# Entering a batch's v tiles term by term, and zeros in planned gaps of the whole early phase, in a planned attention and gated-MLP kernel

## The chip, the core and the metric

One core of a Trainium2 chip. The time of a kernel is the device time in microseconds; several runs are shown by their median. The kernel before has 417.27 us (three runs, 416.51 to 417.78). A measurement of this kernel can tell about 0.3% from no change, which is 1.25 us.

## What is computed

Local and global attention, then a gated MLP on its output, in float32 for 4 batches, 8 heads of 64, 768 positions:

```python
scores = scale * np.matmul(q, k.transpose(0, 1, 3, 2))
scores = np.where(keep, scores + bias, -1e9)        # keep: 8 global keys, or the 96 before
a = np.exp(scores - scores.max(-1)); a = a / (a.sum(-1) + 1e-09)
x = heads_side_by_side(np.matmul(a, v))             # (B, 768, 512)
h = gelu(x @ w_in)                                  # tanh form, 1024 columns
u, v = h[..., :512], h[..., 512:]
v_n = (v - v.mean(-1)) / np.sqrt(v.var(-1) + 1e-06) * g_ln
v_s = np.einsum('ts,bsd->btd', w_sg, v_n) + b_sg[None, :, None]
out = x + (u * v_s) @ w_out
```

## The kernel before

**Attention** goes in units of one batch, one pair of heads and 256 positions: 12 units a batch, 48 in all, numbered from 0 in the order of `units` (256 positions first, then the four pairs). `step` issues for a unit: the scores of a unit three ahead (L831, in quarters of the array, into two PSUM banks `s_ps`), its softmax (`softmax`: DVE adds the bias and takes the extreme at L863, ACT takes the exponent at L868, DVE the reciprocal at L881, and the four parts of `p` are scaled at L888 on ACT, L890 on POOL or L893 on DVE), the transposes of `p` (for units below 16 on TensorE at L952, into the bank `tps`, copied to `pt` at L957 on ACT or L958 on DVE), the product with v (L980, banks `av`), and `take`, which copies `av` to `xh` (L1077) and splits it into a high and a low part of the tile `x` (L1089 to L1095). A unit fills the x of its pair of heads and its 256 positions.

**The MLP** multiplies in three terms (high by high, high by low, low by high), so that each product over 128 rows is three matmuls, L500, L501 and L502, from `Moe.terms`. Per batch there are six v tiles (128 positions by 512 columns, four products over the pairs of heads, 12 matmuls each, bank `mm_ps`), u tiles, mix tiles (w_sg by the normalised v, named `z`) and output tiles. Behind a v tile stands its gelu (`gelu2`: L519 on ACT, L521 on DVE, L523 on ACT, L524 on DVE), then the norm (L558 to L560 on DVE, L563 on POOL, L565 on DVE) and the split into `z` (L534 and L538). Weights come in 64-bit floats and are turned into pairs by `load_split` (L665 on ACT, L668 to L672 on DVE, L675 or L676, and L677).

**The order.** `phase` interleaves units with MLP tiles in source order; every operation goes to `Plan`, which tries 40 random sets of priorities against its own costs, gives each operation an engine (some can run on two or three) and a place, and writes the best order down engine by engine. What is emitted is a fixed order on each of PE, ACT, DVE, POOL and SP. A tile whose product waits for data at its first term only is set by `behind`: with 0, the first term waits for all pairs' x (L506 to L518). Batch 0 has three phases of four units: no tiles in the first, v tiles 0 and 1 in the second, 2 and 3 in the third; v tiles 4 and 5 lead the first phase of batch 1, followed by the u tiles and the mix tiles.

**Zeros.** Where the planner sees TensorE idle for 0.6 us or more ahead of an operation that opens a bank, before 29 us, `keep_on` (L443 to L450) multiplies zeros into that bank, as many as `zeros` works out from the planned gap. The zeros are read from the first part of `bsg`, the place of a bias vector, which is therefore loaded only after 30 us (`w.vectors.since`).

Of the kernel before, what the change touches and what calls it, by code (L numbers as in the profile page):

```python
# [13 lines left out]
BF16 = mybir.dt.bfloat16  # L14
# [5 lines left out]
P = 128  # L20
# [3 lines left out]
FF = 512  # L24
NT = S // P
KD = DM // P
# [31 lines left out]

APART = 0.2

IDLE, ON_UNTIL = 0.6, 29.0

SPARE, SPARE_LATE = 2, 0

# [147 lines left out]
class Plan:  # L212
# [231 lines left out]
    def keep_on(self, o):  # L444

        to = next((b for b in o.bufs if b.kind == "bank" and b.ops[0] is o), None)
        n = o.banks
        for _ in range(self.zeros(o)):
            self.tc.nc.tensor.matmul(to[:, 0:n], self.on[:, 0:P], self.on[:, 0:n], start=True,
                                     stop=True)  # L450

    def emit(self, start):
# [24 lines left out]
class Moe:  # L477
# [62 lines left out]
        op([on_dve_sb(n) + (lambda: lo(nc.vector),), on_pool(n) + (lambda: lo(nc.gpsimd),)],  # L540
           [src, (out, 0)], [(out, 1)])

    def v_tile(self, x, t):
        w = self.w
        c, ts = t * P // CH, ds(t * P % CH, P)
        return self.terms(
            KD, FF, lambda k: ((x[k][c][:, 0, ts], x[k][c][:, 1, ts]),
                               (w.win[:, 0, k, FF:], w.win[:, 1, k, FF:])),
            lambda k: [(x[k][c], t), (w.win, (k, 2))], 0, partial(self.norm, t))

    def norm(self, t, ps):
        nc, w, op = self.nc, self.w, self.plan.op
# [130 lines left out]
def local_global_attention_moe(tc, qk_in, v_in, q_t, k_t, v_n, n_gl, w_in, g_ln, w_sg_t, b_sg,  # L683
# [5 lines left out]
    w = Weights()  # L689
# [16 lines left out]
    w.g = wp.tile([P, KD], F32, name="g")  # L706
    w.bsg = wp.tile([P, S], F32, name="bsg")

    on = w.bsg.bitcast(BF16)[:, 0:FF]
    nc.vector.memset(on, 0.0)  # L710
    xp = fast.enter_context(tc.tile_pool(name="x", bufs=1))
    zp = fast.enter_context(tc.tile_pool(name="z", bufs=1))
# [389 lines left out]
    w.wsg = Buf(lambda _: wp.tile([P, 2, NT, S], F32R, name="wsg"))  # L1102
    w.wout = Buf(lambda _: wp.tile([P, 2, KD, DM], F32R, name="wout"))
    w.vectors = Buf(None)
    w.vectors.since = ON_UNTIL + 1.0

    def load_vectors():
        op([("SP", 0.38, 0.3, lambda: nc.sync.dma_start(
# [113 lines left out]
    def flat(*lists):  # L1222
        return [x for todo in lists for x in todo]
# [11 lines left out]
    for b in range(B + 1):  # L1235
        n0 = [(b * NU + u) * NPAIR for u in range(NU)]
        ns = [range(a, a + NPAIR) if b < B else [] for a in n0]
        if b < B:
            moe = Moe(nc, w, (zp, tp), bank, plan)
            x, dst = X(b), out[b]  # L1240
            cur = ([moe.v_tile(x, t) for t in range(NT)],
                   {(c, j): moe.u_tile(x, c, j) for c in range(NCH) for j in range(KD)},
                   {(c, j): moe.mix_tile(c, j) for c in range(NCH) for j in range(KD)},
                   [[moe.out_tile(x, c, m, dst, b == B - 1 and c == NCH - 1) for m in range(KD)]
                    for c in range(NCH)])
        if b == 0:
            phase(ns[0], [], w_v)
            load_vectors()
            phase(ns[1], flat(*cur[0][0:2]), w_u[:4])
            phase(ns[2], flat(*cur[0][2:4]), w_u[4:] + w_s[0][:3])  # L1250
        else:
            v, u, mix, o = prev
            lead = flat(v[4], v[5], u[0, 0], u[0, 1], mix[0, 0], u[0, 2], mix[0, 1], u[0, 3],
                        mix[0, 2], mix[0, 3])
            late = w_s[0][3:] + w_o[0] + w_o[1] + w_s[1] if b == 1 else []
            if b < B:
                phase(ns[0], lead + flat(u[1, 0], *o[0]), late)
                phase(ns[1], flat(u[1, 1], mix[1, 0], u[1, 2], mix[1, 1], u[1, 3], mix[1, 2],
                                  mix[1, 3]))
                phase(ns[2], between(cur[0][0:4], o[1]))  # L1260
            else:
                phase([], lead + flat(u[1, 0], *o[0], u[1, 1], mix[1, 0], u[1, 2], mix[1, 1],
                                      u[1, 3], mix[1, 2], mix[1, 3]))
                phase([], [t[k] for k in range(KD) for t in o[1][:3]] + o[1][3])
        prev = cur
        if b == 1:
            general = cp.tile([P, 1], I32, name="general")
            op([("DVE", 0.9, 1.0, find_general)], [xs[b, 0, 0]], [])
# [154 lines left out]
```

## Time and profile before

| | us |
|---|---|
| median of three runs | 417.27 |
| the profiled execution | 415.91 |
| its span, first to last instruction | 414.1 |
| TensorE busy | 401.4 (97%) |
| VectorE (DVE) busy | 320.1 (77%) |
| ScalarE (ACT) busy | 232.2 (56%) |
| GpSimd (POOL) busy | 165.5 (40%) |
| mean granted TensorE clock | 0.989 of full speed |

The profiled execution is 1.36 us below the median of the runs, and 1.81 us of its time lie outside the span. Shares over the whole span hide that the stages differ: up to some 60 us of the span the units' softmax runs on ACT and DVE with little for TensorE to do, after 70 us TensorE has work all the time.

### The profile page before, as it was taken

The page shows a single profiled execution, that of the slowest core. Times are in us where ns is not written, and L with a number is a line of the kernel's source. Part 1 is how long each engine was busy: PE and PEld are TensorE (multiplying, and loading weights), DVE is VectorE, ACT ScalarE, POOL GpSimd, SP SyncE. Part 2 cuts the span into 40 slices and gives each one's busy share as a digit, 9 for nine tenths or more (in the row PEclk, how much of TensorE's full clock was granted, in tenths as well). Part 3 has the DMA queues.
Part 4 walks back from the last instruction along what each step waited for, and adds up shares of the span by engine and source line. Part 5 has one row for each costly group of instructions (what it writes and reads, how often), then busy time and mean ns, then how long its engine had stood idle before and what let it go on. Part 6 is the DMA issues. An engine that isn't in the chain of part 4 may idle for free.

```text
span 414.1 us, 12552 instructions
## 1 busy us (share of the span) xinstructions
PE 401.4 (97%) x4638; PEld 365.4 (88%) x4638; DVE 320.1 (77%) x1053; ACT 232.2 (56%) x777; POOL 165.5 (40%) x312
## 2 busy tenths in 40 slices
PE   8989979999999999999999999999999999999994
PEld 5867768989999888999999888999999888999994
DVE  6897897999976899987666899967657788753462
ACT  5999997987777664654245555644235234321220
POOL 3425553673645437233355237533453122203100
PEclk9999987999999999999999999999999999999998
DMA  7954773236889686726778575616756501001002
GB/s 224 299 185 141 232 228 100 97 122 210 269 258 285 192 245 195 214 79 190 214 240 233 181 232 152 199 40 206 235 175 206 186 21 38 2 0 57 20 2 84
DMA packets 50037, 67.17 MB, mean 162 GB/s; under 512 B 5808, under 2 KB 33968, under 8 KB 49968
## 3 DMA queue, kind: packets, MB, share of 16 engines
q1 hardware_dynamic: 49968, 66.28, 52.4%
q8 instruction: 39, 0.64, 0.7%
q14 instruction: 30, 0.25, 0.2%
HBM read 47.91 MB, written 18.35 MB: 160 GB/s over the span
## 4 chain that ended last, share of the span: by engine, by line
PE 77%; DVE 3%; DMA 1%; issue 0%; SPq 0%
PE mm_ps L500 23%; PE mm_ps L502 22%; PE mm_ps L501 22%; PE av L980 6%; PE s_ps L831 5%; DMA pt<-far 1%; DVE vg L565 0%; DVE stage L672 0%; DVE stage L670 0%; DVE st L558 0%; DVE vg L524 0%; DVE u L524 0%; DVE u L521 0%; DVE stage L668 0%; DVE z L538 0%; DVE vg L521 0%
## 5 line engine op out<-in xcount | busy, mean ns | idle before, releaser
L868 ACT ACTIVATE p<-p,pst 128x168 f32<-128x168 f32 (+1 forms) x192 | 80.9, 424 | 32.1 <-DVE pst L863 30.0
L890 POOL TENSOR_SCALAR p<-p,pst 128x168 f32<-128x168 f32 (+1 forms) x132 | 57.1, 448 | 21.4 <-DVE pst L881 17.2
L500 PE MATMUL mm_ps<-wsg,z 128*128 128x384 f32 x192 | 65.0, 339 | 0.0
L502 PE MATMUL mm_ps<-wsg,z 128*128 128x384 f32 x192 | 64.2, 334 | 0.0
L501 PE MATMUL mm_ps<-wsg,z 128*128 128x384 f32 x192 | 64.2, 334 | 0.0
L863 DVE CUSTOM_DVE_ANT_0 p<-s_ps,bias 128x168 f32<-128x168 f32 (+1 forms) x192 | 52.9, 318 | 3.0 <-PE s_ps L831 1.4
L626 POOL TENSOR_TENSOR o<-o,x 128x384 f32<-128x384 f32 x28 | 28.6, 1024 | 65.2 <-DVE o L623 39.3
L980 PE MATMUL av<-pt,v 64*64 64x128 f32 (+1 forms) x1408 | 49.7, 253 | 1.9 <-ACT pt L957 0.8
L980 PEld LDWEIGHTS av<-pt,v 64*64 64x64 f32 x1408 | 38.3, 135 | 9.9 <-issue 2.9
L500 PE MATMUL mm_ps<-x,win 128*128 128x384 f32 x128 | 43.6, 341 | 0.0
L502 PE MATMUL mm_ps<-gt,wout 128*128 128x384 f32 x128 | 42.9, 336 | 0.0
L500 PE MATMUL mm_ps<-gt,wout 128*128 128x384 f32 x128 | 42.9, 335 | 0.0
L502 PE MATMUL mm_ps<-x,win 128*128 128x384 f32 x128 | 42.9, 335 | 0.0
L501 PE MATMUL mm_ps<-gt,wout 128*128 128x384 f32 x128 | 42.8, 335 | 0.0
L501 PE MATMUL mm_ps<-x,win 128*128 128x384 f32 x128 | 42.8, 334 | 0.0
L534 ACT CAST gt<-y 128x384 fp32r<-128x384 f32 x29 | 14.8, 511 | 49.3 <-DVE y L595 38.1
L831 PE MATMUL s_ps<-qk 64*64 64x104 f32 (+2 forms) x1408 | 40.0, 243 | 0.6 <-DVE u L524 0.5
L500 PE MATMUL mm_ps<-win,x 128*128 128x512 f32 x96 | 40.6, 423 | 0.0
L919 DVE STREAM_TRANSPOSE tt<-p 128x384 f32<-128x384 f32 (+1 forms) x64 | 33.3, 544 | 7.7 <-DMA far<-tt 4.9
L831 PEld LDWEIGHTS s_ps<-qk 64*64 64x64 f32 x1408 | 34.5, 136 | 5.1 <-issue 2.5
L502 PE MATMUL mm_ps<-win,x 128*128 128x512 f32 x96 | 38.1, 397 | 0.0
L501 PE MATMUL mm_ps<-win,x 128*128 128x512 f32 x96 | 38.1, 397 | 0.0
(109 smaller groups left out, 904.1 us busy)
## 6 DMA issues: line engine op xcount, KB each, us to landing
qk<-in_qk_in_dram SPq DMA_DIRECT2D x32, 328.0 KB, 3.8
far<-tt SPq DMA_DIRECT2D x96, 96.0 KB, 3.0
pt<-far SPq DMA_DIRECT2D x24, 384.0 KB, 4.1
v<-in_v_in_dram SPq DMA_DIRECT2D x32, 256.0 KB, 4.3
out_dram<-o SPq DMA_DIRECT2D x32, 192.0 KB, 2.2
qk<-in_qk_in_dram SPq DMA_DIRECT2D x16, 276.0 KB, 3.7
v<-in_v_in_dram SPq DMA_DIRECT2D x16, 192.0 KB, 3.3
far<-tt SPq DMA_DIRECT2D x32, 80.0 KB, 3.0
```

Of the source, the lines that this page charges most:

```text
L500: mm(ps.ap, ah, bh, start=(i == 0), stop=False)
L501: mm(ps.ap, ah, bl, start=False, stop=False)
L502: mm(ps.ap, al, bh, start=False, stop=(i == n - 1))
L534: put(out[:, 0, :], src.ap)
L626: lo = lambda eng: eng.tensor_tensor(o.ap, o.ap, xm[:, 1, :].bitcast(F32), ALU.add)
L831: nc.tensor.matmul(s_ps[h][e * HQ:(e + 1) * HQ, i * W + c0:i * W + c0 + n], qk[rows, qc:qc + HQ], qk[rows, QW + k0:QW + k0 + n], start=Tru ...
L863: nc.vector.tensor_tensor_reduce(out=p[:, g, cols], in0=s_ps[h][:, i * W:i * W + nk], in1=bias[:, 2 * j + h, w0:w0 + nk], op0=ALU.add, op1 ...
L868: op([on_act(nk, 0.225) + (lambda p=p, g=g, cols=cols, i=i: nc.scalar.activation(p[:, g, cols], p[:, g, cols], AF.Exp, bias=st[:, 0, i, g: ...
L890: op([on_pool_ts(nk, -0.10) + (partial(scaled, lambda o, a, c: nc.gpsimd.tensor_scalar(o, a, c, 1.0, ALU.mult, ALU.mult)),), on_act(nk, 0. ...
L919: nc.vector.transpose(out, src.rearrange("p g (b j) -> p g b j", j=QB))
L980: nc.tensor.matmul(to, v[rows, vc:vc + D], of, stop=True, skip_group_check=True, **kw)
```

## The change

Five edits. (1) The v tiles of batch 0 get `behind = 3`, so that each of their four terms waits for its own pair's x alone. (2) Their terms are entered one phase earlier, and by pairs of tiles, term by term: tiles 0 and 1 in the first phase, 2 and 3 in the second, 4 and 5 in the third, instead of whole tiles a phase later. (3) The lead of batch 1 no longer holds v tiles. (4) Zeros may be planned up to 75 us instead of 29. (5) They are read from one column of its own, repeated over all columns by a stride of nothing, so that `bsg` may be loaded at any time.

```diff
-IDLE, ON_UNTIL = 0.6, 29.0
+IDLE, ON_UNTIL = 0.6, 75.0
...
-            self.tc.nc.tensor.matmul(to[:, 0:n], self.on[:, 0:P], self.on[:, 0:n], start=True,
+            self.tc.nc.tensor.matmul(to[:, 0:n], self.on.to_broadcast([P, P]), self.on.to_broadcast([P, n]), start=True,
                                      stop=True)
...
-    def v_tile(self, x, t):
+    def v_tile(self, x, t, behind=0):
...
-            lambda k: [(x[k][c], t), (w.win, (k, 2))], 0, partial(self.norm, t))
+            lambda k: [(x[k][c], t), (w.win, (k, 2))], behind, partial(self.norm, t))
...
-    on = w.bsg.bitcast(BF16)[:, 0:FF]
+    on = cp.tile([P, 1], BF16, name="on")
...
-    w.vectors.since = ON_UNTIL + 1.0
...
-            cur = ([moe.v_tile(x, t) for t in range(NT)],
+            cur = ([moe.v_tile(x, t, 0 if b else KD - 1) for t in range(NT)],
...
-            phase(ns[0], [], w_v)
+            phase(ns[0], flat(*zip(*cur[0][0:2])), w_v)
             load_vectors()
-            phase(ns[1], flat(*cur[0][0:2]), w_u[:4])
-            phase(ns[2], flat(*cur[0][2:4]), w_u[4:] + w_s[0][:3])
+            phase(ns[1], flat(*zip(*cur[0][2:4])), w_u[:4])
+            phase(ns[2], flat(*zip(*cur[0][4:6])), w_u[4:] + w_s[0][:3])
...
-            lead = flat(v[4], v[5], u[0, 0], u[0, 1], mix[0, 0], u[0, 2], mix[0, 1], u[0, 3],
+            lead = flat(*(v[4:6] if b > 1 else ()), u[0, 0], u[0, 1], mix[0, 0], u[0, 2], mix[0, 1], u[0, 3],
```

The planner draws anew, so the written order changes on every engine. Three places of it matter below.

TensorE where the early phase ends, before. `tps_1410` and `tps_1414` take the transposes of unit 13, `mm_ps_1388` is v tile 4 of batch 0, `x_700` to `x_1029` are the x of the four pairs:

```order
L980 MATMUL av_1351<-pt_1329,v_1244 64x128
L500 MATMUL mm_ps_1388<-win_347,x_837 128x512
L501 MATMUL mm_ps_1388<-win_347,x_837 128x512
L502 MATMUL mm_ps_1388<-win_347,x_837 128x512
L952 MATMUL tps_1410<-ident_102,p_120 128x128 x2
L952 MATMUL tps_1414<-ident_102,p_121 128x128 x3
L500 MATMUL mm_ps_1388<-win_347,x_908 128x512
L501 MATMUL mm_ps_1388<-win_347,x_908 128x512
L502 MATMUL mm_ps_1388<-win_347,x_908 128x512
```

The same place in the change; `tps_1430` and `tps_1440` are unit 13, `mm_ps_1448` is the first u tile:

```order
L980 MATMUL av_1384<-pt_1359,v_1295 64x128
L952 MATMUL tps_1430<-ident_103,p_121 128x128 x2
L952 MATMUL tps_1440<-ident_103,p_122 128x128 x3
L500 MATMUL mm_ps_1448<-x_380,win_354 128x384
L501 MATMUL mm_ps_1448<-x_380,win_354 128x384
L502 MATMUL mm_ps_1448<-x_380,win_354 128x384
```

Before, 18 v matmuls (half of tile 4 and tile 5) stand between the transposes of unit 13 and the first u tile; now none does.

ACT at the scaling of unit 13's `p` (statistics `pst_1252` before), before:

```order
L1089 CAST x_1029<-xh_1325 128x256
L665 ACTIVATE stage_1175<-stage_1175 128x256
L665 ACTIVATE stage_1081<-stage_1081 128x256
L665 ACTIVATE stage_1124<-stage_1124 128x256
L888 ACTIVATE p_121<-p_121,pst_1252 128x168
L888 ACTIVATE p_120<-p_120,pst_1252 128x128
```

ACT at the same place in the change (`pst_1255`); `vg_1379` is the gelu of v tile 4, `wsg` and `win` are weights:

```order
L675 CAST wsg_1194<-stage_1330 128x384
L519 ACTIVATE vg_1379<-mm_ps_1133 128x512
L675 CAST win_354<-stage_1214 128x256
L888 ACTIVATE p_121<-p_121,pst_1255 128x128
L675 CAST win_354<-stage_1261 128x256
L888 ACTIVATE p_121<-p_121,pst_1255 128x128
L523 ACTIVATE vg_1379<-vg_1379 128x512
L888 ACTIVATE p_122<-p_122,pst_1255 128x168
```

The gelu of a fifth v tile and five casts of weights now stand ahead of the last scaling of unit 13.

TensorE in the first phase, in the change: v tiles 0 (`mm_ps_420`) and 1 (`mm_ps_433`), by the x of pairs 0 and 1, around the transposes of unit 2:

```order
L502 MATMUL mm_ps_420<-win_354,x_380 128x512
L500 MATMUL mm_ps_433<-win_354,x_380 128x512
L501 MATMUL mm_ps_433<-win_354,x_380 128x512
L502 MATMUL mm_ps_433<-win_354,x_380 128x512
L952 MATMUL tps_443<-ident_103,p_119 128x128 x2
L952 MATMUL tps_447<-ident_103,p_120 128x128 x3
L500 MATMUL mm_ps_420<-win_354,x_430 128x512
L501 MATMUL mm_ps_420<-win_354,x_430 128x512
```

Both tiles hold a bank from here to after unit 3; before, no v matmul stood in this phase, and a v tile was opened when all its x was there.

## Rows read from the trace of the kernel before

**Rows 1.** Busy time by stretch: start and end of the stretch and its length in us, then the busy us of PE, PEld, DVE, ACT and POOL with their instructions, the granted clock (1.00 is full), the DMA share and GB/s.

```profile
10.00:20.00 10.00, 9.82 (x218) 8.20 (x217) 8.49 (x39) 10.00 (x40) 5.46 (x13) 1.00 0.92 312
20.00:30.00 10.00, 8.24 (x171) 6.51 (x170) 9.93 (x38) 9.97 (x37) 2.44 (x4) 1.00 0.57 174
30.00:40.00 10.00, 10.00 (x177) 7.86 (x180) 7.59 (x39) 9.99 (x40) 4.65 (x13) 1.00 0.50 156
40.00:50.00 10.00, 9.44 (x211) 7.19 (x201) 8.46 (x37) 10.00 (x40) 6.17 (x10) 1.00 0.66 208
50.00:60.00 10.00, 8.21 (x143) 6.05 (x140) 9.41 (x38) 9.91 (x36) 4.99 (x9) 1.00 0.85 251
...
70.00:80.00 10.00, 10.00 (x104) 9.11 (x104) 9.55 (x32) 9.93 (x34) 8.00 (x12) 1.00 0.52 159
80.00:90.00 10.00, 9.52 (x101) 8.52 (x100) 9.97 (x33) 8.54 (x28) 5.98 (x9) 1.00 0.34 109
90.00:100.00 10.00, 10.00 (x106) 9.75 (x106) 9.86 (x31) 8.01 (x25) 4.89 (x7) 1.00 0.58 188
100.00:110.00 10.00, 10.00 (x67) 9.83 (x59) 9.59 (x31) 8.05 (x26) 4.96 (x8) 1.00 0.74 214
```

**Rows 2.** Whom TensorE waited for over the whole span: us in total, times, longest.

```profile
PE tps L952 <- ACT p L888: 2.1, 3, 1.1
PE s_ps L449 <- DVE bsg L710: 1.2, 1, 1.2
PE tps L952 <- POOL p L890: 1.1, 1, 1.1
PE av L980 <- ACT pt L957: 0.8, 2, 0.6
PE av L980 <- DVE pt L958: 0.7, 1, 0.7
PE s_ps L831 <- DVE u L524: 0.5, 1, 0.5
```

**Rows 3.** TensorE in order of time, a run of zeros, and where the early phase ends: start, duration, line, operation, operands, count, and in brackets the idle time before it and who ended it.

```profile
11.08 0.78 PE L449 MATMUL av<-bsg 128*128 128x128 bf16 x11
...
29.56 0.55 PE L952 MATMUL tps<-ident,p 128*128 128x128 f32 x3 [1.06 <-POOL p L890]
...
57.93 0.44 PE L952 MATMUL tps<-ident,p 128*128 128x128 f32 x2 [1.06 <-ACT p L888]
58.94 0.55 PE L952 MATMUL tps<-ident,p 128*128 128x128 f32 x3 [0.57 <-ACT p L888]
...
60.58 0.80 PE L980 MATMUL av<-pt,v 64*64 64x128 f32 x8 [0.74 <-DVE pt L958]
...
63.05 0.79 PE L500 MATMUL mm_ps<-win,x 128*128 128x512 f32 x1
...
65.77 1.23 PE L952 MATMUL tps<-ident,p 128*128 128x128 f32 x5
66.69 0.54 PE L500 MATMUL mm_ps<-win,x 128*128 128x512 f32 x1
...
70.95 0.33 PE L500 MATMUL mm_ps<-x,win 128*128 128x384 f32 x1
```

**Rows 4.** Single microseconds there, columns as in Rows 1.

```profile
57.00:58.00 1.00, 0.07 (x1) 0.08 (x2) 1.00 (x3) 0.91 (x5) 1.00 (x2) 1.00 0.87 311
58.00:59.00 1.00, 0.42 (x3) 0.19 (x4) 1.00 (x4) 1.00 (x4) 0.24 (x2) 1.00 0.81 230
...
60.00:61.00 1.00, 0.42 (x6) 0.42 (x8) 1.00 (x6) 1.00 (x5) 0.93 (x1) 0.50 0.48 157
...
66.00:67.00 1.00, 1.00 (x6) 1.00 (x5) 0.00 (x0) 0.00 (x0) 0.00 (x0) 0.58 0.00 0
```

**Rows 5.** ACT in order of time at the scaling of unit 13's `p` (L888) and at the copy of its transposes (L957).

```profile
60.98 1.11 ACT L665 ACTIVATE stage<-stage 128x256 f32<-128x256 f32 x3
61.98 0.72 ACT L888 ACTIVATE p<-p,pst 128x168 f32<-128x168 f32 x2
...
67.04 0.75 ACT L957 COPY pt<-tps 128x384 f32<-128x384 f32 x2 [2.56 <-PE tps L952]
```

**Rows 6.** ACT's groups over the span, shapes apart: count, busy us in all, mean ns of one, idle time before them.

```profile
L888 ACT ACTIVATE p<-p,pst 128x168 f32<-128x168 f32 x43 | 16.6, 429 | 2.3 <-DVE pst L881 2.1
L523 ACT ACTIVATE vg<-vg 128x512 f32<-128x512 f32 x24 | 15.1, 630 | 6.9 <-DVE vg L521 6.8
L519 ACT ACTIVATE vg<-mm_ps 128x512 f32<-128x512 f32 x24 | 14.2, 593 | 14.6 <-PE mm_ps L502 10.8 <-POOL o L626 1.9 <-issue 1.8
L957 ACT COPY pt<-tps 128x384 f32<-128x384 f32 x21 | 9.4, 473 | 2.6 <-PE tps L952 2.6
L1077 ACT COPY xh<-av 128x128 f32<-128x128 f32 x32 | 7.4, 264 | 2.7 <-PE av L980 2.6
L675 ACT CAST wsg<-stage 128x384 fp32r<-128x384 f32 x8 | 4.1, 508 | 0.2 <-DMA stage<-in_w_sg_t_dram 0.2
L888 ACT ACTIVATE p<-p,pst 128x128 f32<-128x128 f32 x8 | 3.1, 397 | 0.0
L675 ACT CAST win<-stage 128x256 fp32r<-128x256 f32 x8 | 2.9, 409 | 0.7 <-DVE stage L672 0.7
```

**Rows 7.** The zeros' weight loads, one for each zero matmul: count, durations ns (least, median, most), first and last start in us.

```profile
L449 PEld LDWEIGHTS <-bsg x102: 95/98/147, 1.2 to 25.6; 128*128 128x128 bf16 x102
```

## The prediction

> **What bounds the kernel now.** I read the busy time by stretch first, then TensorE's waits, then TensorE and ACT in order of time where the one stage turns into the other. By stretch [rows 1] the kernel has two stages. From 10 to 60 us ACT has 9.91 to 10.00 us of work in every 10; TensorE looks as busy in places, but part of that is multiplied zeros, 102 of them up to 25.6 us [rows 7], and part is waiting. From 70 us TensorE is full, 10.00 of 10 but for one gap, and stays so to the end. So the first stage lasts as long as ACT needs, the second as long as TensorE's remaining matmuls take. The waits say the same: of TensorE's waits that reach half a microsecond in total, all but the one for `u` lie in the first stage, and most end at something ACT, DVE or POOL did for the softmax or the transposes [rows 2].
>
> The seam is the place to read closely [rows 3]. TensorE waits 1.06, 0.57 and 0.74 us before units 12's transposes and product. After that thin stretch (busy 0.07 and 0.42 us in the microseconds from 57 to 59) its granted clock is 0.50 from 60 until about 66.6 us [rows 4], which is the 1.2 GHz level. So the first six matmuls of v tiles 4 and 5 take 65.77 - 63.05 = 2.72 us. The transposes of unit 13 follow at 65.77, then the other 18 v matmuls from 66.69, and the first u matmul starts at 70.95. ACT meanwhile is through with unit 13's `p` at 61.98 + 0.72 = 62.70 and later sits idle 2.56 us until the transposes come [rows 5]. That is what there is to win: TensorE does here, late and partly at half clock, work that ACT's stage had room for.
>
> **The yardstick.** The order of the changed kernel holds, from the first u matmul on, the same matmuls as before: 384 of u, 720 of mix, 480 of output, 216 v matmuls of the later batches and the same units. Before, this remainder takes 414.1 - 70.95 = 343.15 us. So the new time is when the first u matmul starts, plus 343.15, plus new waits behind it.
>
> **The change, part by part.**
> *The v matmuls moved* cost nothing new: all 72 are still there. What leaves the seam is 18 of them, 70.95 - 66.69 = 4.26 us at full clock, and the six at half clock come one unit earlier. Where they go, TensorE has zeros and waits to give. Taking the 5.9 us of waits [rows 2] and half of the 6.6 us at half clock out of 70.95, TensorE alone could be at the u tiles at 61.7; it does not set the new date.
> *The ACT work moved* does. In the new order the last scaling of unit 13's `p` stands behind more ACT work than before. I counted ACT's instructions up to it in both orders. A count times the mean duration would be too much, since neighbours overlap: three L665 of some 0.44 us take 1.11 us, two L888 of 0.429 take 0.72 [rows 5, 6]. So I take 0.1 us off each. More: 5 copies L1077 at 0.16 (0.82), one L519 and one L523 of a fifth v tile (0.49 + 0.53), three casts of `win` at 0.31 (0.93) and two of `wsg` at 0.41 (0.82), four scalings of 128 columns at 0.30 (1.19), three copies of three transposes at 0.37 (1.12). Fewer: seven scalings of 168 columns at 0.33 (-2.30). These give 3.60. Small items without a row here (one more L665 and one exponent with its read-out, one copy of two transposes, three short and one fewer long split L1089) add some 1.3 by the same reckoning. Sum 4.9 us. ACT has no idle time to put them in, so that scaling ends at 62.70 + 4.9 = 67.6 instead of 62.70. Three transposes behind it last 0.55 [rows 3], so the first u matmul can start at 68.15. ACT's 2.56 us of idle time is used up.
> *Waits that come on top.* The order chains ACT to DVE and POOL just ahead of that scaling (the gelu's L521, the reciprocal, two low halves on POOL). No row shows how that meets; the nearest rows are TensorE's single waits of 0.5 to 1.06 us [rows 2, 3], and I take one of 0.5, since the new chain has the same links as the old. A negative wait is ruled out by ACT's order.
> *Zeros.* 84 instead of 102. Past 29 us the order has only two runs, five of 384 columns and nine of 128, each ahead of transposes or a product that waits for ACT anyway; eleven of 128 columns last 0.78 us [rows 3], 0.07 each, so nine last 0.6. Cost nothing, as long as the wait they fill is there; if it isn't, they delay unit 11 by that much.
> *The column of its own.* The same matmul on the same zeros. That reading one column again and again costs more is shown by no row; the bounds are nothing and double of each, which for the 47 narrow ones is 47 x 0.07 = 3.3 us and for the 37 wide ones, by their columns, some 8 us. I take nothing, because the runs stand in waits and only what outlasts a wait counts; what did would act as rival A does.
> *The loads.* On SP's queue `bsg` (384 KB) and the second stage of w_in move ahead of loads of `qk` and `v`. ACT's stage shows no wait for a DMA now; taken as nothing.
> *Behind the seam.* The mix tiles follow the u tiles sooner, and from 70 to 110 us DVE has 9.55 to 9.97 us of work in 10 [rows 1]. But the new order gives DVE less: 15 instead of 21 products of L595 and 32 instead of 40 low halves of L538, the other 14 on POOL, which is busy 4.9 to 8.0 in 10. I take nothing for it.
>
> **The sum.** 68.15 + 0.5 + 343.15 = 411.8 us of span against 414.1: 2.3 us less. The profiled execution has 415.91 and the median of the runs 417.27; with the same difference to the median, **414.9 us**.
>
> **The rivals.** "About the same" is within 1.25 us, what a measurement of this kernel can tell.
> *A. The early units starve (slower).* v tiles 0 to 3 are opened as soon as the first pair's x is there and hold two of eight banks each time for a whole phase of four units, while scores three units ahead want two banks a unit. If scores then wait for banks, ACT gets its exponents late and idles, and every such wait goes straight into the date of the u tiles. For it: ACT's stage has no slack at all. Against it: the planner counts banks when it writes the order. Five waits of 1.06 us (the longest there is [rows 3]) would be 5.3: 68.15 + 5.3 + 343.15 = 416.6 of span, or 419.8. It decides against the change from 2.8 us of lost ACT time, and makes it measurably slower from 4.1.
> *B. The clock falls again (about the same).* The new order changes between matmuls of the whole array and quarters 40 times before the u tiles, not 30, so TensorE's work is in smaller pieces. If it again thins out before 60 us, a stretch like 60 to 66.6 costs half its length, 3.3 us, on top: 418.2. Against it: TensorE waited 1.06 us before 29.56 and the clock stayed at 1.00 [rows 1, 3], and the v matmuls now fill the thin places. The Trainium skill, "TensorE: Matmul & The Clock Gate", section "A second HAM failure mode: psum-queue depth-cycling", says that frequent short idle times between groups of matmuls make the clock swing between its levels; by that rule this rival would be the likely case and the time 418.2. The waits before 43 us in this trace did not do it, so I follow the rows.
> *C. The gain is given back behind the seam (about the same).* Mix tiles wait for z of tiles 4 and 5 or for w_sg, with DVE as the bound. DVE's free time from 70 to 110 us is 40 - 38.97 = 1.03 us [rows 1]; if nothing were taken off it, only that much of the gain could stay: 416.3.
> *D. ACT's surplus hides (faster).* If the moved ACT work falls in time that only looks full, the transposes of unit 13 end at 66.69 as now and all of 4.26 us is won: 413.0.
> *E.* That the edit does nothing is excluded for the order; that it does nothing for the time, 0.02.
>
> **How the numbers follow.** Forecast 0.52 (within it, nearly all is faster by over 1.25 us, since it takes 1.1 us more of waits to lose that), A 0.12, B 0.09, C 0.15, D 0.10, E 0.02. Faster: 0.48 + 0.10 + 0.04 of C = 0.62. About the same: 0.04 + 0.09 + 0.10 + 0.02 = 0.25. Slower: A and a little of C, 0.13. The range goes from D, 413.0, to 417.8, inside B and below A; what it leaves out is most of A, part of B and little below D. The forecast's own range is 413.9 to 416.0.
>
> **What would show it.** Right: the first u matmul near 68.5 us with no v matmul of batch 0 behind unit 13's transposes; the transposes' second half ended by ACT's L888; ACT full from 10 to 68 us; granted clock 1.00 from 50 to 70; and the stretch from there to the end within half a microsecond of 343.15. Wrong: idle time of ACT before 60 us behind L863 (A); a clock of 0.50 after 50 us (B); waits of mix matmuls for z or w_sg between 70 and 110 (C); the first u matmul before 67.6, where ACT's order would not have set the date (D).

## The result, and the profile after

The changed kernel is **slower by 0.5%**: 418.56 us (median of 20 runs, 416.66 to 421.01) against 416.12 us (20 runs, 413.87 to 419.68), ratio 1.0053, 95% interval 1.0032 to 1.0073. The forecast was 414.9, with a range of 413.0 to 417.8. The profiled execution has 416.94 us and a span of 415.2, so it is 1.6 us under its median, while the one of before (415.91) lies close to its own. A single pair of traces shows no more than part of the 2.4 us, and below I compare several executions of each order.

The changed kernel by stretch, from 10 to 110 us, columns as in [rows 1]:

```profile
10.00:20.00 10.00, 9.50 (x156) 7.38 (x155) 9.10 (x32) 9.82 (x36) 4.27 (x7) 1.00 0.86 297
20.00:30.00 10.00, 9.24 (x149) 6.84 (x148) 7.80 (x35) 9.68 (x38) 4.87 (x10) 1.00 0.47 135
30.00:40.00 10.00, 9.66 (x162) 6.65 (x163) 8.32 (x38) 9.10 (x34) 5.37 (x14) 1.00 0.30 91
40.00:50.00 10.00, 9.76 (x197) 7.73 (x200) 5.84 (x28) 9.72 (x38) 6.95 (x12) 1.00 0.57 185
50.00:60.00 10.00, 9.30 (x177) 6.75 (x170) 9.40 (x37) 10.00 (x39) 4.47 (x9) 1.00 0.60 173
60.00:70.00 10.00, 9.18 (x136) 6.32 (x134) 9.69 (x38) 9.45 (x35) 5.74 (x9) 1.00 0.63 192
70.00:80.00 10.00, 9.63 (x94) 9.38 (x97) 9.81 (x32) 10.00 (x34) 6.40 (x8) 1.00 0.76 225
80.00:90.00 10.00, 10.00 (x126) 9.01 (x119) 9.60 (x31) 8.35 (x31) 7.44 (x13) 1.00 0.39 123
90.00:100.00 10.00, 10.00 (x108) 9.54 (x107) 9.67 (x27) 7.57 (x23) 8.72 (x11) 1.00 0.49 147
100.00:110.00 10.00, 8.77 (x106) 8.31 (x106) 9.81 (x33) 6.90 (x25) 5.88 (x8) 1.00 0.69 216
```

Three things differ from [rows 1]. The clock is 1.00 all the way; [rows 1] leave out 60 to 70 us, which in the kernel before reads

```profile
60.00:70.00 10.00, 9.42 (x71) 7.86 (x72) 7.42 (x26) 7.25 (x25) 3.09 (x6) 0.66 0.26 80
```

ACT, the fourth column of busy times, is no longer full before 60 us: from 10 to 70 us it is idle for 2.23 us, 0.90 of them between 30 and 40, where the kernel before had 0.13 us from 10 to 60. And VectorE has 38.89 us of work from 70 to 110 us, against 38.97 before: of the 14 instructions that it gives to POOL only two stand in this stretch (L595 two instead of three, L538 four instead of five), 1.2 us, and other work fills their place.

TensorE at the seam in the changed kernel, which answers to [rows 3, 4]:

```profile
65.77 0.50 PE L500 MATMUL mm_ps<-win,x 128*128 128x512 f32 x1 [0.51 <-DVE x L1091]
...
69.52 0.44 PE L952 MATMUL tps<-ident,p 128*128 128x128 f32 x2 [0.27 <-DVE xh L1078]
70.37 0.44 PE L952 MATMUL tps<-ident,p 128*128 128x128 f32 x2 [0.41 <-ACT p L888]
70.56 0.43 PE L500 MATMUL mm_ps<-x,win 128*128 128x384 f32 x1
```

The last row is the first u matmul: 70.56 us, against 70.95 before and 68.65 in the forecast. The row ahead of it shows the order of events that was forecast, transposes of unit 13 whose wait ends with ACT's scaling; the first u matmul is 1.9 us later than forecast. ACT's waits from 10 us to that scaling, and the scaling itself (last row), which answer to [rows 5]:

```profile
21.91 0.44 ACT L868 ACTIVATE p<-p,pst 128x168 f32<-128x168 f32 x1 [0.32 <-DVE pst L881]
38.33 0.43 ACT L888 ACTIVATE p<-p,pst 128x168 f32<-128x168 f32 x1 [0.65 <-DVE pst L881]
39.01 0.43 ACT L1077 COPY xh<-av 128x128 f32<-128x128 f32 x2 [0.25 <-PE av L980]
43.55 0.76 ACT L888 ACTIVATE p<-p,pst 128x168 f32<-128x168 f32 x2 [0.24 <-DVE pst L881]
61.62 0.69 ACT L888 ACTIVATE p<-p,pst 128x128 f32<-128x128 f32 x2 [0.17 <-DVE pst L881]
66.95 0.41 ACT L675 CAST win<-stage 128x256 fp32r<-128x256 f32 x1 [0.38 <-DVE stage L672]
...
69.89 0.43 ACT L888 ACTIVATE p<-p,pst 128x168 f32<-128x168 f32 x1
```

TensorE's waits over the whole span, which answer to [rows 2]; the transfers now lead:

```profile
PE av L980 <- DMA pt<-far: 1.8, 2, 1.2
PE s_ps L449 <- DVE on L710: 1.0, 1, 1.0
PE av L980 <- ACT pt L957: 0.9, 2, 0.7
PE mm_ps L500 <- DVE x L1091: 0.9, 2, 0.5
```

And those behind the seam in order of time, where the kernel before had two, 0.48 and 0.31 us:

```profile
108.02 0.68 PE L980 MATMUL av<-pt,v 64*64 64x128 f32 x24 [1.23 <-DMA pt<-far]
122.77 0.45 PE L501 MATMUL mm_ps<-wsg,z 128*128 128x384 f32 x1 [0.34 <-DVE wsg L677]
166.29 0.50 PE L980 MATMUL av<-pt,v 64*64 64x128 f32 x10 [0.61 <-DMA pt<-far]
```

`pt<-far` is the second hop of a transpose that units from 16 on make through VectorE (L919), a write of `tt` to memory (L927) and a read back (L931). These 2.18 us in place of 0.79 are nearly the whole lengthening of the remainder in this pair of traces: 415.2 - 70.56 = 344.64 us against 343.15.

### The profile page after: what moved, and what is told of

Same layout as the page of the kernel before. It is cut to its first block, busy times and chain, and to the rows that moved or that the text cites. A ratio compares the mean times of both kernels' runs of the same rounds, so it can differ in the third digit from the quotient of the medians.

```text
span 415.2 us, 12517 instructions
## 1 busy us (share of the span) xinstructions
PE 402.4 (97%) x4620; PEld 362.4 (87%) x4620; DVE 312.6 (75%) x1023; ACT 233.1 (56%) x780; POOL 190.6 (46%) x339
## 4 chain that ended last, share of the span: by engine, by line
PE 79%; DVE 8%; ACT 4%; DMA 3%; POOL 2%; issue 2%; SPq 1%; DVEq 0%; POOLq 0%
PE mm_ps L500 22%; PE mm_ps L502 21%; PE mm_ps L501 21%; PE av L980 7%; PE s_ps L831 5%; PE tps L952 2%; DMA far<-tt 2%; ACT p L868 1%; DVE p L863 1%; DVE tt L919 1%; POOL p L890 1%; DMA pt<-far 1%; DMA v<-in_v_in_dram 1%; ACT p L888 1%; DVE stage L672 1%
## 5 line engine op out<-in xcount | busy, mean ns | idle before, releaser
L890 POOL TENSOR_SCALAR p<-p,pst 128x168 f32<-128x168 f32 (+1 forms) x142 | 63.9, 467 | 24.4 <-DVE pst L881 23.3
L980 PE MATMUL av<-pt,v 64*64 64x128 f32 (+1 forms) x1408 | 48.8, 251 | 2.7 <-DMA pt<-far 1.8
L980 PEld LDWEIGHTS av<-pt,v 64*64 64x64 f32 x1408 | 37.4, 134 | 11.9 <-issue 5.4
L919 DVE STREAM_TRANSPOSE tt<-p 128x384 f32<-128x384 f32 (+1 forms) x64 | 33.4, 545 | 10.0 <-DMA far<-tt 8.0
L831 PE MATMUL s_ps<-qk 64*64 64x64 f32 (+2 forms) x1408 | 39.8, 241 | 0.8 <-DMA qk<-in_qk_in_dram 0.6
L534 ACT CAST gt<-y 128x384 fp32r<-128x384 f32 x31 | 15.8, 510 | 39.3 <-DVE y L595 23.6
```

The costliest lines, as they stand in the source:

```text
L534: put(out[:, 0, :], src.ap)
L831: nc.tensor.matmul(s_ps[h][e * HQ:(e + 1) * HQ, i * W + c0:i * W + c0 + n], qk[rows, qc:qc + HQ], qk[rows, QW + k0:QW + k0 + n], start=Tru ...
L890: op([on_pool_ts(nk, -0.10) + (partial(scaled, lambda o, a, c: nc.gpsimd.tensor_scalar(o, a, c, 1.0, ALU.mult, ALU.mult)),), on_act(nk, 0. ...
L919: nc.vector.transpose(out, src.rearrange("p g (b j) -> p g b j", j=QB))
L980: nc.tensor.matmul(to, v[rows, vc:vc + D], of, stop=True, skip_group_check=True, **kw)
```

## Experiments

Every kernel was timed in five rounds against the kernel before on the same chip; the ratio is to that. "First u" is the start of the first u matmul, "last" that of the last MLP matmul, and "behind" the time between, so that the tail of output writes is left out; "waits" are TensorE's between the two. These four are from the one profiled execution of each kernel, the median and the ratio from all its runs. Kernels that keep every engine's written order are marked "order kept"; the others make the planner draw again.

| kernel | us | ratio, 95% | first u | last | behind | waits behind |
|---|---|---|---|---|---|---|
| before, profiled | 416.12 | 1 | 70.95 | 408.09 | 337.14 | 0.79 |
| b_light, order kept | 415.95 | 0.9949-1.0013 | 68.95 | 407.40 | 338.45 | 1.80 |
| b_far, order kept | 417.70 | 0.9997-1.0051 | 70.06 | 409.32 | 339.26 | 2.02 |
| b_recip, order kept | 416.63 | 0.9975-1.0029 | 68.47 | 408.14 | 339.67 | 2.67 |
| b_sg, order kept | 416.44 | 0.9958-1.0015 | 69.61 | 407.11 | 337.50 | 1.16 |
| b_dve, order kept | 417.10 | 0.9989-1.0049 | 70.84 | 409.11 | 338.27 | 1.61 |
| b_z75 | 416.01 | 0.9973-1.0012 | 68.73 | 406.54 | 337.81 | 1.15 |
| changed, profiled | 418.56 | 1.0032-1.0073 | 70.56 | 409.49 | 338.93 | 2.18 |
| a_z29, order kept but for zeros | 417.76 | 1.0012-1.0071 | 70.55 | 410.65 | 340.10 | 2.78 |
| a_light, order kept | 417.89 | 0.9994-1.0047 | 70.33 | 411.01 | 340.68 | 2.79 |
| a_far, order kept | 419.62 | 1.0039-1.0117 | 70.54 | 411.03 | 340.49 | 2.79 |
| a_recip, order kept | 418.65 | 1.0016-1.0068 | 70.60 | 410.70 | 340.10 | 2.97 |
| a_sg, order kept | 418.18 | 1.0005-1.0054 | 70.59 | 411.29 | 340.70 | 2.38 |
| a_dve, order kept | 417.58 | 0.9990-1.0033 | 70.42 | 410.23 | 339.81 | 2.21 |

### The zeros, each way

a_z29 takes the late zeros out of the changed kernel; b_z75 turns the same number round in the kernel before, with the column of its own and `bsg` free to load as in the change.

```diff
-IDLE, ON_UNTIL = 0.6, 75.0
+IDLE, ON_UNTIL = 0.6, 29.0
```

> The changed kernel with zeros planned only up to 29 us, so without the last 14 zeros; its order is otherwise word for word that of the change. If the late zeros cost time (they outlast their waits): first u matmul up to 1 us earlier than 70.6 and a ratio to the kernel before of 1.001 to 1.003 instead of 1.005. If they hold the clock: a granted clock of 0.50 appears somewhere between 50 and 70 us and the ratio goes to 1.008 or more. If they do nothing: ratio 1.004 to 1.006.

> The kernel before with the zeros alone: planned up to 75 us, read from one column, bias vector free to load early; v tiles entered as before. The planner draws anew. If the half clock at the seam is what the zeros cure and nothing else changes: no 0.50 between 60 and 66.6, first u matmul near 67.7, ratio 0.992 to 0.995. If the draw decides: ratio anywhere from 0.99 to 1.01, with new waits to be seen behind the seam.

a_z29 differs from the changed kernel by nothing that can be measured, the first u matmul starts at 70.55 and the mean clock is 0.996. What the zeros had filled is now waiting:

```profile
35.19 0.55 PE L952 MATMUL tps<-ident,p 128*128 128x128 f32 x3 [1.30 <-DVE vg L524]
...
60.80 0.88 PE L980 MATMUL av<-pt,v 64*64 64x128 f32 x15 [0.51 <-ACT pt L957]
```

So the late zeros do nothing in this order that shows, for the clock or for the time. b_z75 drew a new order, without half clock, and brings the first u matmul to 68.73 us, where my forecast for the change had it (not to 67.7, as expected if nothing but the half clock changed). In the pair of traces its last matmul comes 1.55 us earlier than that of the kernel before (406.54 against 408.09), so 0.7 of the 2.2 us gained at the seam is lost again; the median time is that of the kernel before. Behind its seam stand these waits of 0.64 and 0.36 us:

```profile
74.92 0.78 PE L980 MATMUL av<-pt,v 64*64 64x128 f32 x10 [0.64 <-ACT u L523]
...
81.08 0.44 PE L502 MATMUL mm_ps<-wsg,z 128*128 128x384 f32 x1 [0.36 <-DVE z L538]
```

### What holds ACT ahead of the seam: a_light, b_light, a_recip, b_recip

The first pair shortens VectorE's instructions on batch 0's v tiles, L521, L524, L558 and L565, to 64 of 512 columns, and so leaves most of that arithmetic out; the second lets ACT's scalings multiply by a constant instead of the reciprocal. The orders stay.

```diff
-        self.gelu2(g, ps, FF)
+        self.gelu2(g, ps, FF, m := 64 if self.first else FF)
...
-            nc.vector.bn_stats(st.ap, g.ap)
+            nc.vector.bn_stats(st.ap, g[:, 0:m])
...
```

```diff
-                    put(ps[i][:, g, cols], ps[i][:, g, cols], st[:, 2, i, g:g + 1])
+                    put(ps[i][:, g, cols], ps[i][:, g, cols], w.mhalf if put == nc.scalar.mul else st[:, 2, i, g:g + 1])
```

> The changed kernel with every engine's order as it is, but VectorE's part of the v tiles of batch 0 on 64 columns instead of 512 (the gelu's two products, the statistics and the normalising; it leaves most of that arithmetic out). Some 448 columns less in four instructions of five tiles: by 0.68 us for 512 columns and 0.42 for 256, about 1.9 us less of DVE per tile. Theory 'DVE holds ACT' (the first u tile is 1.9 us later than forecast because ACT's scalings wait 2.0 us in all for reciprocals that stand on DVE behind the v tiles' arithmetic, 0.65 of it in one place behind the statistics of two tiles): the first u matmul comes at 68.3 to 69.2 us instead of 70.56, the waits of ACT for the reciprocal between 20 and 45 us go. Rival 'ACT's own chain' (the exponents, the sum on POOL and the reciprocal take that long whatever DVE does): first u matmul at 70.2 or later, the waits stay. The time behind the seam may gain as well, since two tiles' z come earlier.

> The same lightening of VectorE in the kernel before, its order unchanged. In its trace ACT is full from 10 to 60 us and waits for no reciprocal, so both theories expect the first u matmul close to 70.95 us (70.3 to 71.2; a little earlier at most, where units 12's transposes waited for scalings). Theory 'DVE holds ACT': the lightening moves the seam by at least 1 us more in the changed kernel than here. Rival: about as little in both.

> The changed kernel, every engine's order as it is, but ACT's scalings of p (L888) multiply by a constant instead of the reciprocal, so that ACT waits for no reciprocal there (the parts of p that ACT scales then hold other numbers). Theory 'ACT's own chain' (exponents on ACT, the sum on POOL, the reciprocal on DVE, the scaling on ACT, with nothing on ACT in between at the places that the new order drew; 1.4 us of waits in all, and lightening DVE took only 0.2 us off the seam): the first u matmul at 69.0 to 69.7 us instead of 70.56. Rival 'another wait takes over' (ACT then waits for TensorE's av, as it already did more when DVE was lightened): 70.0 to 70.5. Either way the end moves less than the seam, if what stands behind the seam sets the time: fall in time under 0.5 us.

> The same in the kernel before, where ACT shows no wait for a reciprocal between 10 and 70 us. Both theories: first u matmul within 0.5 us of 70.95, or earlier by what the half clock ahead of it happens to last, and the time as before within 0.3%.

The first u matmul of the changed order did not move: 70.33 and 70.60. "VectorE holds ACT" and "ACT's own chain" both fall, and "another wait takes over" holds. In a_light ACT waits 0.27 instead of 0.65 us for the reciprocal, and 0.71 instead of 0.25 for `av`; in a_recip it waits for no reciprocal at all there, and then this:

```profile
39.07 0.43 ACT L1077 COPY xh<-av 128x128 f32<-128x128 f32 x2 [0.99 <-POOL rs L563]
```

That copy starts at 39.01, 39.15 and 39.07 us in the three kernels. It needs the last part of a product with v (L980). Between that product's two parts the order that was drawn puts six v matmuls and another unit's scores. TensorE in a_recip:

```profile
35.73 0.68 PE L980 MATMUL av<-pt,v 64*64 64x128 f32 x24
36.34 0.50 PE L500 MATMUL mm_ps<-win,x 128*128 128x512 f32 x1
...
37.93 0.82 PE L831 MATMUL s_ps<-qk 64*64 64x104 f32 x32
38.57 0.40 PE L980 MATMUL av<-pt,v 64*64 64x128 f32 x8
```

TensorE has no idle time from 35.73 to 38.97, where the last part ends. The row of a_recip names POOL's L563, which ended at 39.04, at nearly the same time; in the changed kernel and in a_light the same copy waits for TensorE's `av`. So 0.9 of ACT's 2.2 idle us (0.65 and 0.25 in the changed kernel) would stay without the wait for the reciprocal: TensorE comes to the product only behind v matmuls that were entered early. That is read from the trace; a kernel without them at that place was not run.

The b kernels show something else. In all six executions with the old order TensorE's work ahead of the seam is the same, but the granted clock from 60 to 70 us is 0.66 (before), 0.83 (b_light), 0.83 (b_far), 0.83 (b_sg), 0.67 (b_dve) and, in b_recip, 1.00. The seam follows it, from 70.95 to 68.47 us; b_light's came 2 us earlier, which I had not expected. b_recip, stretches from 60 us, and its wait behind the seam:

```profile
60.00:70.00 10.00, 9.26 (x86) 7.81 (x86) 9.67 (x41) 9.95 (x36) 5.57 (x9) 1.00 0.46 131
70.00:80.00 10.00, 10.00 (x119) 8.99 (x117) 9.86 (x28) 9.99 (x33) 6.82 (x11) 1.00 0.33 115
```

```profile
68.47 0.33 PE L500 MATMUL mm_ps<-x,win 128*128 128x384 f32 x1
...
117.62 0.68 PE L980 MATMUL av<-pt,v 64*64 64x128 f32 x24 [1.59 <-DMA pt<-far]
```

First u 2.48 us earlier than in the kernel before, last matmul at 408.14 against 408.09: in this pair the earlier seam is worth nothing at the end. That is not a rule. In b_light 2.00 us at the seam are 0.69 at the last matmul, in b_sg 1.34 are 0.98, in b_z75 2.22 are 1.55; in b_far and b_dve the last matmul comes 1.2 and 1.0 us later, though the seam does not. These are single executions of kernels that differ.

The runs of the kernel before itself, beside which the others were timed, speak against it too. Of 135 the span and the mean granted clock are on record. The 43 with a mean clock of 0.992 or less have a median span of 416.0 us, the 42 with 0.996 or more one of 413.5. In the six traces of the old order the clock fell at the seam and behind the last matmul alone, so the mean clock tells mainly how much of the seam ran at 1.2 GHz. This points to an end that moves with the seam by about as much, 2.5 us; where the clock fell in the executions without a trace is not known. At 0.996 or more 19 of the changed kernel's 20 runs have a median span of 416.8, 3.3 us above the kernel before at like clock.

### What paces the stretch behind the seam: a_far, b_far, a_sg, b_sg, a_dve, b_dve

The orders stay. Each edit puts other numbers into the result: the second hop reads an input instead of what the first hop wrote (far); batch 0's mix tiles for the later half of the positions read the first half of w_sg (sg); VectorE does the u tiles' gelu and y times u on 64 of 384 columns (dve).

```diff
-            to[:, :, 0:nt * QB], far[:, :, :, 0:nt * QB].rearrange("b j a f -> (b j) a f")))],
+            to[:, :, 0:nt * QB], qk_in[0, 0, 1][:, 0:nt * QB].rearrange("p (o f) -> p o f", o=1).to_broadcast([P, Q4, nt * QB])))],
```

```diff
-        js = slice(j * P, (j + 1) * P)
+        js, ws = slice(j * P, (j + 1) * P), slice(0, CH) if self.first else cs
...
-                               (w.wsg[:, 0, s, cs], w.wsg[:, 1, s, cs])),
+                               (w.wsg[:, 0, s, ws], w.wsg[:, 1, s, ws])),
```

```diff
-            self.gelu2(u, ps, CH)
+            self.gelu2(u, ps, CH, 64 if self.first else CH)
...
-            op([on_dve_sb(CH) + (lambda: by_u(nc.vector),),
+            op([on_dve_sb(CH) + (lambda m=64 if self.first else CH: nc.vector.tensor_tensor(y[:, 0:m], y[:, 0:m], gt[:, 0:m], ALU.mult),),
```

> The changed kernel, every engine's order as it is, but the second hop of the far transposes (L931) reads an input instead of what the first hop (L927) wrote, so it need not wait for the first to land (the product is then with other numbers). Theory 'given back in the far transfers' (the stretch from the first u matmul to the end is 1.5 us longer than before mainly because products with v wait 1.2 and 0.6 us for transposed p that come late): these waits go, the stretch shrinks from 344.6 to 342.8 to 343.4, and the time falls by 1.2 to 1.8 us, to some 417.0. Rival 'other waits take their place' (VectorE's w_sg and z are as late, and the waits only move to them): the time falls by less than 0.5 us.

> The same in the kernel before, whose trace has one wait of 0.31 us for such a transfer. Theory 'given back in the far transfers': the time falls by 0.3 us or less, so the changed kernel comes closer to it by 1 us or more. Rival: both fall by about the same.

> The changed kernel, every engine's order as it is, but the mix tiles of batch 0's second half of positions read the first half of w_sg, which is there long before (other numbers in them). The loads and their arithmetic stay. Theory 'w_sg holds the date at 123 us': in four executions of the changed order the mix matmul at 121.7 to 123.1 us waited 0.34, 1.36, 0.62 and 0.99 us for VectorE's low half of w_sg, and what an earlier wait gave back was lost there again. So this wait goes, the stretch from the first u matmul to the last matmul shrinks by 0.3 to 1.4 us and the time falls by about 0.8 us to 417.3 or so. Rival 'the next wait takes over': the score or product behind it waits instead (for its transfer), and the time stays within 0.3 us.

> The same in the kernel before, whose three executions with this order show no wait for w_sg: no difference, within 0.3%, under either theory.

> The changed kernel, every engine's order as it is, but VectorE's part of the u tiles' gelu and its products of u and y in batch 0 work on 64 of 384 columns (most of that arithmetic is left out): 22 instructions of 0.55 us lose some 0.35 us each, 7.7 us off VectorE between 70 and 140 us. Theory 'VectorE paces the stretch behind the seam' (it has 9.4 to 10.0 us of work in 10 from 70 to 110 us, so the scalings, stream transposes and low halves of w_sg that stand in its order come late): the waits behind the seam at 107 to 109 us for a far transpose and at 122 to 123 us for w_sg go (1.6 to 2.3 us together), and the time falls by at least 1.2 us, to 417.3 or less. Rival 'the transfers pace it' (one buffer tt, four DMAs a transpose on one queue, the landing): both waits stay within 0.5 us of what they were, time within 0.6 us of 418.5.

> The same in the kernel before (19 instructions, 6.7 us off VectorE). Theory 'VectorE paces it': its waits at 84 and 117 us go and the time falls by 0.5 to 1.5 us, to 415.0 to 416.0. Rival 'the transfers': no difference within 0.6 us.

a_far did not help, nor did b_far: the waits stay or move to w_sg. The median time from issue to landing is 4.6 us for the second hop against 4.3, so the transfer is not gone, and the pair does not settle what the transfers cost. In a_far 0.74 us gained at the first row below is nearly lost again at the second, 0.65:

```profile
107.29 0.68 PE L980 MATMUL av<-pt,v 64*64 64x128 f32 x24 [0.49 <-DMA pt<-in_qk_in_dram]
...
122.96 0.45 PE L501 MATMUL mm_ps<-wsg,z 128*128 128x384 f32 x1 [0.99 <-DVE wsg L677]
```

a_sg has no wait for w_sg, and its time is the changed kernel's within the interval; its profiled execution waited 1.91 us at 108.73 instead. b_sg shows no difference, as expected. a_dve has no wait near 108 us and one of 0.45 at 122. Its ratio, 1.0011, stands against the changed kernel's 1.0053; that is 1.7 us, by the medians alone 1.0, and the two intervals just touch. Its waits behind the seam add up to 2.21 us, as many as the changed kernel's 2.18. Rows of it:

```profile
121.72 0.44 PE L501 MATMUL mm_ps<-wsg,z 128*128 128x384 f32 x1 [0.45 <-DVE wsg L677]
...
124.28 0.68 PE L980 MATMUL av<-pt,v 64*64 64x128 f32 x24 [0.38 <-DMA pt<-far]
```

So that VectorE's load bears on the changed order is possible and not shown; the limit of 417.3 us set for that theory was not reached. b_dve gained nothing, against the theory; there the product still waited for its transfer:

```profile
118.83 0.68 PE L980 MATMUL av<-pt,v 64*64 64x128 f32 x24 [1.28 <-DMA pt<-far]
```

Five of the six executions of the old order wait for a transfer at 117 to 119 us (0.25 to 1.59 us), and b_far for its input there (0.48). None of the three, the transfers, w_sg and VectorE, is shown to be the one cause: in these traces, where one wait goes, another is longer.

### The draw: seeds 2, 3 and 4

```diff
-        rnd = random.Random(1)
+        rnd = random.Random(2)
```

> The changed kernel, the planner's random numbers started from 2 instead of 1. If the early entry itself costs the time (theory edit): ratio near 1.005 again, 1.003 to 1.008, with ACT idle some 2 us between 10 and 70 us. If the plan drawn decides (theory draw): ratio off by more than 0.004 from 1.005, and other waits behind the seam.

> The kernel before, the planner's random numbers started from 2. Theory edit: within 0.3% of the kernel before, half clock at the seam again. Theory draw: 0.990 to 1.010, as far from 1 as the change is.

> The changed kernel with a third set of random priorities in the planner (a seed of 3 instead of 1, nothing else). Theory 'the edit costs' : slower than the third draw of the kernel before by some 2 us, as with the first draw. Theory 'the draw decides': anywhere from 415 to 421, with no fixed sign against the kernel before at the same seed (with the second draw it was 2.2 us faster). Its seam should lie between 69 and 71 us under both.

> The kernel before with the third set of random priorities. Theory 'the edit costs': 415.5 to 417, as with the first. Theory 'the draw decides': anywhere from 415 to 421.

> The changed kernel with a fourth set of random priorities. Theory 'the draw decides, and the first draw of the kernel before was a lucky one': 418 to 420 us, like the other three draws of this order, and faster than the kernel before at the same seed. Theory 'the edit costs': slower than that by about 2 us. An order that beats both kernels would have to come in under 416.

> The kernel before with a fourth set of random priorities. Theory 'the first draw was a lucky one': 419 to 423 us, with more than 3 us of waits of TensorE behind the seam (0.8 to 2.7 with the first draw, 7.1 and 6.7 with the second and third). Theory 'the edit costs': 416 to 417.5.

| seed | before | changed | first u, before / changed | behind | waits behind |
|---|---|---|---|---|---|
| 1 | 1 | 1.0053 | 70.95 / 70.56 | 337.14 / 338.93 | 0.79 / 2.18 |
| 2 | 1.0115 (1.0086-1.0144) | 1.0059 (1.0036-1.0082) | 70.55 / 69.32 | 343.89 / 341.82 | 7.13 / 4.36 |
| 3 | 1.0107 (1.0064-1.0151) | 1.0049 (1.0020-1.0079) | 68.65 / 68.73 | 346.47 / 342.03 | 6.66 / 3.89 |
| 4 | 1.0044 (1.0002-1.0086) | 1.0046 (1.0020-1.0072) | 70.06 / 69.56 | 342.07 / 341.32 | 4.43 / 3.30 |

All are ratios to the kernel before. With seed 1 the change costs 0.5%, with 2 and 3 it gains 0.6% (with 3 the two intervals overlap a little), with 4 it does nothing. The changed kernel is the same with all four, 1.0046 to 1.0059; the kernel before is at 1 with its own draw and between 1.0044 and 1.0115 with the others. a_s2 by itself came out as "the edit costs" had it; against the old order at the same seed that theory falls, and "the draw decides" holds for the sign. The seams of seed 3 came earlier than the 69 to 71 us expected. The date of the seam does not order these kernels: the longest stretch behind it, 346.47 us (seed 3 of before), follows the earliest seam. The two slow ones, seeds 2 and 3 of before, have the most waits behind it, and the clock fell there too, to 0.50 from 84.6 to 91.5 us with seed 2 and from 119.8 to 123.2 with seed 3; the other six lie too close for an order. No version ran that beats both; b_z75 equals the kernel before.

## Why the prediction was wrong

Two terms of the sum failed: 343.15, the yardstick with no new waits behind the seam, and 68.15 + 0.5, ACT's order and the waits on top. The span of the profiled execution is 3.4 us above the 411.8 forecast, 1.9 of it at the seam (70.56 instead of 68.65) and 1.5 behind it.

**The yardstick.** "So the new time is when the first u matmul starts, plus 343.15, plus new waits": I took the 343.15 us of one execution as TensorE's own work and set the new waits at nothing. By the stretch from the first u to the last matmul, that execution has the shortest of all in the table (337.14 us) and the fewest waits (0.79); the other five of its own order have 337.50 to 339.67 us and 1.16 to 2.67 us of waits, and the seven of the changed order 338.93 to 340.70 and 2.18 to 2.97. It was a lucky one: among the 16 runs on record of the kernel before with a mean clock of 0.987 to 0.989 (its own is 0.989, span 414.1) one alone has a shorter span, 413.6. In the changed order the waits are for far transfers and for w_sg. That the units behind the seam keep a pace of their own, so that an earlier seam only makes them wait, is a reading that fits b_recip; the 135 runs of the kernel before speak against it. What sets these waits stays open. (The matmul counts that I gave for mix and output, 720 and 480, are also off: 576 and 384 run.)

**ACT's order and the waits on top.** The direction held, "ACT's order sets the date"; the size did not. The last scaling of unit 13 ends at 69.89 + 0.43 = 70.32 instead of 67.6, 2.7 us later. Up to it ACT has 63.65 us of work, against 57.99 up to 62.70 in the kernel before: 5.66 more instead of the 4.9 that I counted, 0.8 short. The other 2.0 are idle time of ACT (6.67 us up to there against 4.71), for which the sum had only 0.5 us of TensorE's waits, "since the new chain has the same links as the old". It has the same links, but in six places nothing on ACT to cover them, and in one of them v matmuls stand ahead of the product. That the v matmuls moved "cost nothing new" failed there. Seven executions put the seam at 70.33 to 70.60.

**Where before's seam is.** I set 70.95 and its half clock down as the kernel's; they are one execution's. The median of six is 69.84. Medians over each order's executions, variants included, then give: seam 70.55 against 69.84, 0.7 us later; behind it 340.10 against 338.36, 1.7 us longer; last matmul 410.70 against 408.12, 2.6 us later, close to the measured 2.4 us. Of the 1.7 us, 1.1 are waits (2.78 against 1.70). The other 0.6 I cannot place; the changed order switches TensorE between the whole array and quarters 58 times behind the seam and the old one 56 times, which no run tested.

**Zeros, the column, the clock.** Costs of nothing: a_z29 and b_z75 show none, though no run has the column alone. The late zeros' use was nothing too (a_z29). The half clock was gone, and stayed away without them.

**The clock's rule.** The Trainium skill, "TensorE: Matmul & The Clock Gate", section "A second HAM failure mode: psum-queue depth-cycling", warns of a swinging clock behind frequent short idle times. The changed kernel and a_z29 have such waits before 70 us, up to 1.30 us, and a clock of 1.00 there; these traces do not bear the rule out for them. In the old order five of six executions fell to 0.50 behind three such waits (1.06, 0.57 and 0.74 us in the kernel before, from 57 to 61 us), and b_recip, with 1.00, 0.62 and 0.74, did not.

**The rivals.** The outcome, slower, had a chance of 0.13, nearly all of it as A, units that starve for banks. That is not what happened: ACT does idle, but for reciprocals, for a product behind v matmuls and for an input of a cast. B: no. C, the gain given back behind the seam, at 0.15, is nearest: mix tiles wait for w_sg, with far transfers beside it. But there was hardly a gain to give back in this pair, 0.4 us at the seam, and the new waits went past C's 416.3. Its "DVE as the bound" is not shown (a_dve); that the 14 instructions moved to POOL freed VectorE was wrong for the stretch that counts, since only two stood there. D: no.

## What to carry to other kernels

A stretch that is full in one trace is not yet a constant: before adding it to a sum, look at a second execution of the same order, and at how late its inputs already are. Where a planner draws the whole order anew, compare an edit over several draws: here the draws of the kernel before differ by 1.1%, while the edit makes 0.5% with the first of them. And a chain over three engines costs nothing only where the waiting engine has something else in its order to do meanwhile.

## What was not expected of the hardware

**A small VectorE instruction lasted until POOL's ended.** The addition L879 on four columns took 0.17 us at 149.23 and 1.25 at 60.12. VectorE of the changed kernel:

```profile
16.97 0.70 DVE L879 TENSOR_SCALAR pst<-pst 128x4 f32<-128x4 f32 x1
...
60.12 1.25 DVE L879 TENSOR_SCALAR pst<-pst 128x4 f32<-128x4 f32 x1
...
149.23 0.17 DVE L879 TENSOR_SCALAR pst<-pst 128x4 f32<-128x4 f32 x1
```

POOL at the same times:

```profile
16.60 1.04 POOL L1095 TENSOR_TENSOR x<-xh,x 128x256 fp32r<-128x256 f32 x1 [2.85 <-DVE stage L672]
...
60.07 1.27 POOL L538 TENSOR_TENSOR z<-vg,z 128x512 fp32r<-128x512 f32 x1 [1.89 <-DVE z L534]
...
149.25 1.29 POOL L538 TENSOR_TENSOR z<-vg,z 128x512 fp32r<-128x512 f32 x1 [2.89 <-DVE z L534]
```

Where POOL had started first, VectorE's addition ends 0.03 us behind it (17.67 against 17.64, 61.37 against 61.34); where VectorE started first, it is short (0.17 us). The trace shows such time as busy, not as a wait. The Trainium skill, "SBUF — State Buffer", section "Who interferes with whom", calls the pair of ports that the two engines share an exclusive lock, held by whichever starts first; the rows agree. That is not so with every instruction of POOL: in b_z75 the addition at 46.04 us began 0.18 us behind a one-column power on POOL (L563), took 0.17 us and ended before it. The lock can be one reason why work moved from VectorE to POOL is not simply off VectorE; how much it was here was not measured.

**The same order, another clock.** Six executions of one written order had from none to 6.8 us of the 1.2 GHz level between 59.8 and 66.8 us, behind nearly the same waits.

**A long wait can cost twice.** In a_sg TensorE waited 1.91 us, and the u matmuls from 111.44 us on then followed each other at 0.32 us, with a granted clock of 0.85 from 110 to 120; after b_recip's wait of 1.59 us the clock stayed at 1.00. a_sg, in order of time and then the stretch:

```profile
108.73 0.68 PE L980 MATMUL av<-pt,v 64*64 64x128 f32 x24 [1.91 <-DMA pt<-far]
...
111.44 0.52 PE L502 MATMUL mm_ps<-x,win 128*128 128x384 f32 x1
111.76 0.52 PE L500 MATMUL mm_ps<-x,win 128*128 128x384 f32 x1
```

```profile
110.00:120.00 10.00, 10.00 (x67) 9.67 (x60) 6.39 (x24) 5.71 (x20) 6.18 (x14) 0.85 0.81 227
```
